# Token blocks of 512 columns in place of 464, and the two layers run one behind the other

## The chip, the cores and the metric

The kernel runs on one core of one Trainium2 chip. The metric is device time in microseconds (us), the median of 3 runs: 1123.47 us before the change (1122.75 to 1123.68). Where one execution was profiled, its own time is given beside it.

The engines in the text: PE is TensorE (matmuls; PEld is its weight load, which runs beside the matmuls), DVE is VectorE, ACT is ScalarE, POOL is GpSimd, SP is SyncE, whose queue issues every DMA of this kernel.

## The reference

Three stages over N = 6016 tokens with C = 256 channels and F = 2048 hidden columns:

```python
def _attn_ref(q, k, v, tau):                      # q, k, v: (1, 6016, 256)
    qn = q / (np.linalg.norm(q, axis=1, keepdims=True) + 1e-06)
    kn = k / (np.linalg.norm(k, axis=1, keepdims=True) + 1e-06)
    s = kn.transpose(0, 2, 1) @ qn / tau          # 256 x 256, sums over tokens
    a = softmax of s over its last axis
    return v @ a

def _moe_ref(x, w_in, w_out):                     # layer 0 of the kernel
    h = x @ w_in                                  # 6016 x 2048
    return (h - np.tanh(h)) @ w_out               # 6016 x 256

def _moe2_ref(x, w_in, w_out):                    # layer 1, with weights of its own
    h = x @ w_in
    g = np.where(h > 0.0, h, np.exp(np.minimum(h, 0.0)) - 1.0)
    return g @ w_out
```

The weights arrive as 8-byte floats. The kernel turns them into pairs of 4-byte numbers (a rounded high part and a rest), and does the same with every matmul operand, so that a product is three matmuls in the format fp32r: high by high, high by low, low by high.

## The kernel before

**Attention.** q and k are read once, their 256 x 256 product S is summed over tokens, and the softmax a is made from it. a is never applied to v: it is multiplied into layer 0's first weight matrix ("fold", the tiles `aw`), so layer 0 reads v directly.

**Blocks and units.** The tokens lie along the free dimension, in blocks of `width` = 464 columns: 12 of 464 and one of 448, 13 in all. For each layer and block there are NP = 8 units, p = 0 to 7, each for 256 of the 2048 hidden columns. A unit has 24 matmuls of one block's width: 12 that make h (`emit_h`, L404 by way of `product`) and 12 that add g @ w_out into the block's output o (`emit_out`, L572). Every matmul has a weight load of its own. Between them `emit_act` makes g on ACT and DVE: layer 0 with one tanh on ACT (L491) and a subtraction on DVE (L492), layer 1 with three ACT passes (L507 to L509) and two DVE passes (L511, L515). Both then take the high part (ACT L503, or DVE L501 and L519) and the rest (DVE L520).

**Order of the work.** The program is written out by hand in issue order; each engine runs its instructions in that order. The list `order` names the units. `LAG = 2`: on PE the out matmuls of a unit follow the h matmuls of the unit two later. h has two PSUM tiles in turn, so the h matmuls of a unit wait until DVE has read the h of two units before.

Before the change the first five p of blocks 0 and 1 alternate (`SIDE = NP - 3`), then come the rest of both, then block 2, and from there units of layer 1 for block b alternate with units of layer 0 for block b + 3 (`interleaved`). Three blocks of layer 1's input stay in SBUF as high and low parts (`xpool`, three buffers): `emit_evac` makes the high part on ACT (L588) and the rest on DVE (L589) from o in PSUM. Layer 0's own input comes by `load_v` from DRAM and is split by `split_v` (ACT L206, DVE L207).

**Conversions.** `Converter` runs beside the units, one weight piece per unit (two where `ticks` is 2): DMA, two ACT passes (L104, L105), four DVE passes (L121, L127, L133, L140), one ACT pass (L158) and one POOL pass (L165). The first converter ("early") has layer 0's weights and the first matrix of layer 1 in pieces of 512 columns, the second ("late") the last matrix of layer 1 in pieces of 256. Between them lies a switch: the SBUF room of the first is given to the second, so that the second's first DMA waits for the last POOL pass of the first, and an ACT pass on it stands in ACT's queue ahead of the unit's tanh.

**Fold.** From p = 1 on, the fold of a p (12 matmuls of 256 columns) stands in PE's queue shortly before the first unit that needs it.

Of the kernel before, what the change touches and what calls it, by code (L numbers as in the profile page):

```python
# [16 lines left out]
P = 128  # L17
# [5 lines left out]
def kernel(  # L23
# [25 lines left out]
    width = 464  # L49
# [17 lines left out]
    class Converter:  # L67
# [122 lines left out]

    v_of = {}

    def load_v(b):
        t0, n = blocks[b]
        raw = vpool.tile([P, KC, width], F32, tag="vraw", name=f"vraw{b}", bufs=1)
        nc.sync.dma_start(
            out=raw[:, :, :n], in_=vT[:, t0 : t0 + n].rearrange("(k p) t -> p k t", p=P)
        )
        v_of[b] = raw

    def split_v(b):
        _, n = blocks[b]
# [180 lines left out]
    with tc.manual_schedule():  # L383
# [5 lines left out]
        xpool = ctx.enter_context(tc.tile_pool(name="x", bufs=3, side="left"))  # L389
        gpool = ctx.enter_context(tc.tile_pool(name="g", bufs=2, side="left"))  # L390
        spool = ctx.enter_context(tc.tile_pool(name="s", bufs=2, side="left"))
        spool_e = ctx.enter_context(tc.tile_pool(name="e", bufs=1, side="left"))
# [46 lines left out]
        x_of = {}  # L439
# [20 lines left out]
        def emit_act(layer, b, p, h, ticks, fold):  # L460
# [43 lines left out]
            else:  # L504

                e = (late_pool[0] if late_pool else spool_e).tile([P, 2, width], F32, tag="e", name="e")[:, :, :n]
# [41 lines left out]
        def emit_last_evac(b):  # L548
            t0, n = blocks[b]
            o = o_of.pop((1, b))[:, :, :n]  # L550
            s = late_pool[0].tile([P, 2, width], F32, tag="osb", name="osb")[:, :, :n]
# [28 lines left out]
        def emit_evac(layer, b, p):  # L580
# [3 lines left out]
            o = o_of.pop((layer, b))[:, :, :n]  # L584
            if layer == 0:
# [3 lines left out]
                nc.vector.tensor_tensor(  # L589
                    out=x_lo[:, :, :n], in0=o, in1=x_hi[:, :, :n].bitcast(F32), op=ALU.subtract  # L590
                )
                x_of[b] = (x_hi, x_lo)
            else:
                s = late_pool[0].tile([P, 2, width], F32, tag="osb", name="osb")[:, :, :n]
                nc.scalar.activation(out=s, in_=o, func=AF.Copy)
# [4 lines left out]
        def interleaved(first, second, lead):  # L600

            first = [(*first, p) for p in range(NP)]
            second = [(*second, p) for p in range(NP)]
            units = []
            while first or second:
                if first:
                    units.append(first.pop(0))
                if second and (not first or len(first) <= NP - lead):
                    units.append(second.pop(0))
            return units  # L610


        order = [(0, b, p) for p in range(SIDE) for b in range(2)]
        order += [(0, b, p) for b in range(2) for p in range(SIDE, NP)]
        order += [(0, 2, p) for p in range(NP)]
        for b in range(NBLK - 3):
            order += interleaved((1, b), (0, b + 3), 1)
        order += interleaved((1, NBLK - 3), (1, NBLK - 2), 4)
        order += [(1, NBLK - 1, p) for p in range(NP)]

# [10 lines left out]
        for s, (layer, b, p) in enumerate(order):  # L631
            ticks = 1 + (s in (14, 18))
            if conv is not early and conv.done() and not late_pool:
                late_stack.close()
                pool = ctx.enter_context(tc.tile_pool(name="o", bufs=2, side="right"))
                late_pool.append(pool)
            if conv is early and early.done():
# [25 lines left out]
            if layer == 0 and b + 1 == nv and nv < NBLK:  # L663
                if p == 1:
                    load_v(nv)
                if p == (5 if b == 1 else 4):
                    split_v(nv)
                    nv += 1
# [38 lines left out]
```

## Time and profile before

| What | Before |
|---|---|
| device time, median of 3 runs | 1123.47 us |
| profiled execution, its own time | 1123.31 us |
| its span, first to last instruction | 1121.3 us |
| PE busy | 1109.8 us (99%), 5360 matmuls |
| DVE busy | 851.1 us (76%) |
| ACT busy | 554.9 us (49%) |
| mean granted TensorE clock | 0.998 of full speed |
| DMA | 42.30 MB, 38 GB/s on average |

How to read it: PE is the engine with almost no idle time, but its busy time counts matmuls with modelled ends that overlap, so it does not tell how fast the matmuls follow each other. That is read from their starts: the distance from one matmul's start to the next, called pace below. The other engines have idle time and matter only where PE waits for them. The profiled execution is 0.16 us under the median of the runs shown.

### The profile page before, as it was taken

The numbers are of one execution on the slowest core, as the hardware profiler recorded it, in microseconds if no ns is written. First come the engines' busy times: TensorE is split into PE (matmuls) and PEld (weight loads), VectorE is DVE, ScalarE is ACT, GpSimd is POOL, SyncE is SP. The second block draws the span as 40 slices with busy tenths as digits, with TensorE's granted clock in tenths as the row PEclk, the third lists the DMA queues.
The fourth block names the chain that finished last, engine by engine and source line by source line (L and its number), as shares of the span: only waits on it lengthen the run. The fifth ranks groups of instructions, "written<-read, shape, count | busy, mean of one in ns | idle before, by whom it ended". The sixth has DMA issues, their size and how long they took to land.

```text
span 1121.3 us, 13606 instructions
## 1 busy us (share of the span) xinstructions
PE 1109.8 (99%) x5360; PEld 992.0 (88%) x5360; DVE 851.1 (76%) x957; ACT 554.9 (49%) x662; POOL 75.0 (7%) x57
## 2 busy tenths in 40 slices
PE   9999999999999999999999999999999999999998
PEld 8789988888888888888888888888888889998897
DVE  6899997998666676667666776667766776678776
ACT  7776666664344334344444434443444443456564
POOL 6422212211000000000000000000000000000000
PEclk9999999999999999999999999999999999999999
DMA  9643221211001001001001001001000000000000
GB/s 350 238 130 92 78 73 57 69 43 34 1 1 35 1 1 35 1 1 34 1 1 34 1 1 34 1 1 35 1 23 12 1 18 1 1 18 1 7 28 17
DMA packets 23040, 42.30 MB, mean 38 GB/s; under 512 B 1984, under 2 KB 8896, under 8 KB 22976
## 3 DMA queue, kind: packets, MB, share of 16 engines
q1 hardware_dynamic: 22976, 41.43, 11.1%
q8 instruction: 42, 0.69, 0.3%
q14 instruction: 22, 0.18, 0.1%
HBM read 35.26 MB, written 6.16 MB: 37 GB/s over the span
## 4 chain that ended last, share of the span: by engine, by line
PE 89%; DVE 6%; issue 2%; ACT 2%; DMA 1%; SPq 0%; POOL 0%; ACTq 0%; DVEq 0%; POOLq 0%
PE h L404 42%; PE o L572 42%; PE S L247 3%; DVE glo L520 1%; PE aw L404 1%; DVE hz L121 1%; DVE cut L140 1%; DVE cut L127 1%; DMA qk<-in_k_dram 1%; DVE g L492 0%; ACT ghi L503 0%; DVE cut L133 0%; DVE g L515 0%; DVE xlo L589 0%; ACT g L491 0%
## 5 line engine op out<-in xcount | busy, mean ns | idle before, releaser
L511 DVE SCALAR_TENSOR_TENSOR g<-e,g 128x928 f32<-128x928 f32 (+1 forms) x103 | 116.8, 1134 | 197.2 <-ACT e L509 197.2
L507 ACT ACTIVATE e<-h 128x928 f32<-128x928 f32 (+1 forms) x103 | 97.3, 944 | 311.2 <-PE h L404 311.2
L520 DVE TENSOR_TENSOR glo<-g,ghi 128x928 fp32r<-128x928 f32 (+1 forms) x207 | 232.4, 1123 | 22.8 <-ACT ghi L503 3.1
L572 PE MATMUL o<-ghi,wout_hi 128*128 128x464 f32 (+1 forms) x832 | 208.8, 373 | 0.1
L572 PE MATMUL o<-glo,wout_hi 128*128 128x464 f32 (+1 forms) x832 | 208.7, 372 | 0.0
L572 PE MATMUL o<-ghi,wout_lo 128*128 128x464 f32 (+1 forms) x832 | 208.5, 372 | 0.0
L491 ACT ACTIVATE g<-h 128x928 f32<-128x928 f32 (+1 forms) x104 | 98.0, 943 | 162.9 <-PE h L404 162.8
L572 PEld LDWEIGHTS o<-glo,wout_hi 128*128 128x128 f32 x832 | 156.2, 188 | 18.9
L572 PEld LDWEIGHTS o<-ghi,wout_lo 128*128 128x128 f32 x832 | 156.3, 188 | 18.2
L572 PEld LDWEIGHTS o<-ghi,wout_hi 128*128 128x128 f32 x832 | 156.2, 188 | 17.7 <-ACT ghi L542 0.4
L404 PE MATMUL h<-vhi,win_hi 128*128 128x464 f32 (+1 forms) x416 | 154.6, 372 | 1.1 <-ACT win_hi L426 0.7
L404 PE MATMUL h<-vlo,win_hi 128*128 128x464 f32 (+1 forms) x416 | 155.1, 373 | 0.0
L404 PE MATMUL h<-xhi,win_hi 128*128 128x464 f32 (+1 forms) x414 | 153.9, 372 | 0.1
L404 PE MATMUL h<-xlo,win_hi 128*128 128x464 f32 (+1 forms) x414 | 153.6, 371 | 0.0
L515 DVE SCALAR_TENSOR_TENSOR g<-h,g 128x928 f32<-128x928 f32 (+1 forms) x103 | 115.5, 1122 | 10.0
L404 PE MATMUL h<-vhi,win_lo 128*128 128x464 f32 (+1 forms) x416 | 120.8, 371 | 0.0
L404 PE MATMUL h<-xhi,win_lo 128*128 128x464 f32 (+1 forms) x414 | 120.0, 370 | 0.0
L492 DVE TENSOR_TENSOR g<-h,g 128x928 f32<-128x928 f32 (+1 forms) x104 | 116.1, 1116 | 1.6 <-ACT g L491 1.4
L508 ACT ACTIVATE g<-e 128x928 f32<-128x928 f32 (+1 forms) x103 | 101.0, 981 | 3.3
L509 ACT ACTIVATE e<-e 128x928 f32<-128x928 f32 (+1 forms) x103 | 100.8, 978 | 3.3
L404 PEld LDWEIGHTS h<-vhi,win_hi 128*128 128x128 f32 x416 | 78.0, 188 | 11.2 <-ACT win_hi L426 0.9
L404 PEld LDWEIGHTS h<-vlo,win_hi 128*128 128x128 f32 x416 | 78.1, 188 | 9.6
(110 smaller groups left out, 1028.7 us busy)
## 6 DMA issues: line engine op xcount, KB each, us to landing
qk<-in_q_dram SPq DMA_DIRECT2D x23, 256.0 KB, 5.1
qk<-in_k_dram SPq DMA_DIRECT2D x23, 256.0 KB, 5.1
vraw<-in_vT_dram SPq DMA_DIRECT2D x12, 464.0 KB, 4.2
out_dram<-osb SPq DMA_DIRECT2D x12, 464.0 KB, 2.9
raw0in<-in_moe_w_in_dram SPq DMA_DIRECT2D x8, 512.0 KB, 3.8
raw0out<-in_moe_w_out_dram SPq DMA_DIRECT2D x8, 512.0 KB, 3.6
raw1in<-in_moe_w_in_dram SPq DMA_DIRECT2D x8, 512.0 KB, 3.7
raw1out<-in_moe_w_out_dram SPq DMA_DIRECT2D x16, 256.0 KB, 2.6
```

The source lines that it names most:

```text
L121: nc.vector.scalar_tensor_tensor(out=hz, in0=s["sq"], scalar=TINY_HIGH**2, in1=s["raw"][:, :, 1].bitcast(F32), op0=ALU.is_ge, op1=ALU.mult,)
L247: nc.tensor.matmul(out=S[m], lhsT=kk[:, 1, j, m * P : (m + 1) * P], rhs=qq[:, 0, j, :], start=(count[m] == 1), stop=(count[m] == total),)
L404: nc.tensor.matmul(out=out, lhsT=w, rhs=x, start=(i == 0), stop=(i == len(pairs) - 1))
L491: nc.scalar.activation(out=g, in_=h, func=AF.Tanh)
L492: nc.vector.tensor_tensor(out=g, in0=h, in1=g, op=ALU.subtract)
L507: nc.scalar.activation(out=e, in_=h, func=AF.Relu, scale=-1.0)
L508: nc.scalar.activation(out=g, in_=e, func=AF.Tanh, scale=-0.5)
L509: nc.scalar.activation(out=e, in_=e, func=AF.Exp, scale=-1.0)
L511: nc.vector.scalar_tensor_tensor(out=g, in0=e, scalar=1.0, in1=g, op0=ALU.add, op1=ALU.mult)
L515: nc.vector.scalar_tensor_tensor(out=g, in0=h, scalar=0.0, in1=g, op0=ALU.max, op1=ALU.add)
L520: nc.vector.tensor_tensor(out=lo, in0=g, in1=hi.bitcast(F32), op=ALU.subtract)
L572: nc.tensor.matmul(out=o[:, c, :n], lhsT=w[layer][:, f, c * P : (c + 1) * P], rhs=x[:, i], start=(f == 0 and w is wout_hi and x is hi), st ...
```

## The change

- `width` becomes 512, so there are 11 blocks of 512 columns and one of 384, 12 in all.
- The layers no longer alternate. `phases` lists all blocks of layer 0 and then all blocks of layer 1; `order` goes through them unit by unit, with blocks 0 and 1 still in pairs, now for all eight p.
- Layer 1's input isn't kept in SBUF. `emit_evac` copies o to an SBUF tile (ACT) and stores it to a DRAM tile `x_dram[b]`; `load_v` later reads it back in place of v, and `split_v` makes high and low part as for layer 0.
- The early converter has layer 0's weights alone, 16 pieces, one per unit; layer 1's 32 pieces of 256 columns all go through the late one, and the switch stands at unit 14. `ticks` is always 1.
- The pool `xpool` goes, the output tile gets a pool of its own with two buffers (`opool`), and the tile e of layer 1 takes two buffers in the room that the late converter leaves.

```diff
-    width = 464
+    width = 512
...
-    SIDE = NP - 3
-    starts = [2 * p if p < SIDE else p + SIDE for p in range(NP)]
+    starts = [2 * p for p in range(NP)]
...
-    NE = 8
-    early_units += [(1, "in", 2 * P * p, 2 * P) for p in range(NE)]
-    wanted = [(2 * p - 1, "in", p) for p in range(NE, NP)] + [(2 * p + 2, "out", p) for p in range(NP)]
     late_units = [
-        (1, which, 2 * P * p + P * i, P) for _, which, p in sorted(wanted) for i in range(2)
+        (1, which, 2 * P * p + P * i, P) for p in range(NP) for which in ("in", "out") for i in range(2)
     ]
...
+    phases = [(layer, b) for layer in range(2) for b in range(NBLK)]
+    dram = ctx.enter_context(tc.tile_pool(name="x", bufs=1, space=bass.MemoryType.DRAM))
+    x_dram = [dram.tile([P, KC, n], F32, name=f"x{b}") for b, (_, n) in enumerate(blocks)]
     v_of = {}
 
-    def load_v(b):
+    def load_v(i):
+        layer, b = phases[i]
         t0, n = blocks[b]
...
+        if layer == 0:
+            src = vT[:, t0 : t0 + n].rearrange("(k p) t -> p k t", p=P)
+        else:
+            src = x_dram[b]
+        nc.sync.dma_start(out=raw[:, :, :n], in_=src)
...
-            x_hi, x_lo = v_of[b] if layer == 0 else x_of[b]
+            x_hi, x_lo = v_of[layer * NBLK + b]
...
+            s = opool.tile([P, 2, width], F32, tag="osb", name="osb")[:, :, :n]
+            nc.scalar.activation(out=s, in_=o, func=AF.Copy)
             if layer == 0:
-                x_hi = xpool.tile([P, KC, width], F32R, tag="xhi", name=f"xhi{b}")
-                x_lo = xpool.tile([P, KC, width], F32R, tag="xlo", name=f"xlo{b}")
-                nc.scalar.activation(out=x_hi[:, :, :n], in_=o, func=AF.Copy)
-                nc.vector.tensor_tensor(
-                    out=x_lo[:, :, :n], in0=o, in1=x_hi[:, :, :n].bitcast(F32), op=ALU.subtract
-                )
-                x_of[b] = (x_hi, x_lo)
+                nc.sync.dma_start(out=x_dram[b], in_=s)
...
+        order = [(0, b, p) for p in range(NP) for b in range(2)]
+        order += [(layer, b, p) for layer, b in phases[2:] for p in range(NP)]
...
-            ticks = 1 + (s in (14, 18))
+            ticks = 1
...
+            if s == 3 or (s > 2 * NP and p == 1 and nv < len(phases)):
+                load_v(nv)
+            if s == 2 * NP - 2 or (s > 2 * NP and p == 4 and nv < len(phases)):
+                split_v(nv)
+                nv += 1
```

How the change moves instructions shows best at two places. The first is PE's queue in the middle of the program, around the first unit of block 5 in layer 0. In the names h0_5_0 is layer 0, block 5, p = 0, and o1_1 is the output of layer 1, block 1; the numbers behind the last underscore only count tiles. Before:

```order
L404 MATMUL h1_2_0_3174<-xhi2_1962,win_lo1_592 128x464 x2
L572 MATMUL o1_1_2703<-ghi_3132,wout_hi1_1758 128x464 x4
L572 MATMUL o1_1_2703<-ghi_3132,wout_lo1_1759 128x464 x4
L572 MATMUL o1_1_2703<-glo_3133,wout_hi1_1758 128x464 x4
L404 MATMUL h0_5_0_3213<-vhi5_2966,win_hi0_61 128x464
```

After (the same statements stand at L407 and L573):

```order
L407 MATMUL h0_4_7_2585<-vhi4_2111,win_lo0_62 128x512 x2
L573 MATMUL o0_4_2363<-ghi_2519,wout_hi0_63 128x512 x4
L573 MATMUL o0_4_2363<-ghi_2519,wout_lo0_64 128x512 x4
L573 MATMUL o0_4_2363<-glo_2520,wout_hi0_63 128x512 x4
L407 MATMUL h0_5_0_2631<-vhi5_2489,win_hi0_61 128x512
```

The neighbour of a layer 0 unit is now the layer 0 unit ahead of it, not one of layer 1, and every matmul has 512 columns; the pattern of 12 and 12 is the same. The second place is ACT's queue at the switch from the early to the late converter, with what each row waits for. Before, in block 2 of layer 0:

```order
L491 ACTIVATE g_1743<-h0_2_5_1718 128x928 [waits PE_49,Activation_49]
L158 ACTIVATE win_hi1_591<-cut_1669 128x2x256
L503 ACTIVATE ghi_1744<-g_1743 128x928 [waits DVE_49,PE_49]
L104 ACTIVATE sq_1772<-raw1out0_1766 128x256 [waits DMAHW5_49,Pool_49]
L105 ACTIVATE low_1773<-raw1out0_1766 128x256
L491 ACTIVATE g_1801<-h0_2_6_1776 128x928 [waits PE_49]
```

After, between the last units of blocks 0 and 1 (L429 is the fold's evacuation, L426 before; L492 the tanh; L504 the high part):

```order
L492 ACTIVATE g_1363<-h0_1_6_1325 128x1024 [waits PE_49]
L429 ACTIVATE win_hi0_61<-aw7_1338,rsum_78 128x256 [waits PE_49,Pool_49]
L429 ACTIVATE win_hi0_61<-aw7_1338,rsum_78 128x256
L158 ACTIVATE wout_hi0_63<-cut_1314 128x512 [waits DVE_49]
L504 ACTIVATE ghi_1364<-g_1363 128x1024 [waits DVE_49,PE_49]
L104 ACTIVATE sq_1396<-raw1in0_1390 128x256 [waits DMAHW4_49,DVE_49,Pool_49]
L105 ACTIVATE low_1397<-raw1in0_1390 128x256
L492 ACTIVATE g_1425<-h0_0_7_1400 128x1024 [waits PE_49]
```

In both the square pass of the late converter's first piece stands ahead of the next unit's tanh, one unit behind the last pass of the early converter; after the change two evacuations of the fold stand there too.

## Rows read from the trace of the kernel before

**Rows 1.** The page, part 1: busy time (share of the span) and instructions.

```profile
PE 1109.8 (99%) x5360; PEld 992.0 (88%) x5360; DVE 851.1 (76%) x957; ACT 554.9 (49%) x662; POOL 75.0 (7%) x57
```

**Rows 2.** The page, part 4: the chain that ended last, by engine.

```profile
PE 89%; DVE 6%; issue 2%; ACT 2%; DMA 1%; SPq 0%; POOL 0%; ACTq 0%; DVEq 0%; POOLq 0%
```

**Rows 3.** Waits of PE, whole span: total us, times, longest us.

```profile
PE aw L404 <- DVE g L492: 1.8, 1, 1.8
```

**Rows 4.** Waits of PE from 76 to 1110 us, all that there are.

```profile
PE h L404 <- DVE g L492: 0.4, 1, 0.4
```

**Rows 5.** The chain in order of time: start us, us, what.

```profile
213.97 2.53 PE o L572 x12
...
914.78 2.52 PE o L572 x12
```

**Rows 6.** Timeline of PE, the last block: start us, us, engine, line, instruction.

```profile
1087.27 0.37 PE L404 MATMUL h<-xhi,win_hi 128*128 128x448 f32 x1
...
1106.79 0.37 PE L404 MATMUL h<-xhi,win_hi 128*128 128x448 f32 x1
```

**Rows 7.** Timeline of PE around one fold.

```profile
84.80 0.28 PE L404 MATMUL aw<-win_hi,aT_hi 128*128 128x256 f32 x1
...
86.22 0.37 PE L572 MATMUL o<-ghi,wout_hi 128*128 128x464 f32 x1
```

**Rows 8.** Windows: length, busy of PE, PEld, DVE, ACT, POOL; PEclk, DMA, GB/s.

```profile
55.30:69.50 14.20, 14.18 (x72) 12.45 (x72) 13.64 (x21) 11.19 (x18) 3.91 (x3) 1.00 0.36 112
72.10:75.50 3.40, 3.40 (x15) 3.23 (x14) 3.37 (x6) 2.58 (x5) 0.00 (x0) 0.50 0.77 287
76.00:145.00 69.00, 69.00 (x357) 62.33 (x356) 66.74 (x85) 48.00 (x74) 15.47 (x12) 1.00 0.31 92
210.00:258.00 48.00, 48.00 (x230) 42.85 (x230) 46.79 (x74) 29.23 (x48) 9.60 (x9) 1.00 0.18 54
1020.00:1105.00 85.00, 85.00 (x410) 76.72 (x410) 67.75 (x69) 50.74 (x54) 0.00 (x0) 1.00 0.03 12
```

**Rows 9.** Timeline of PE behind its longest wait.

```profile
71.65 0.38 PE L404 MATMUL aw<-win_hi,aT_hi 128*128 128x256 f32 x1 [1.80 <-DVE g L492]
...
74.02 1.69 PE L572 MATMUL o<-ghi,wout_hi 128*128 128x464 f32 x4
75.55 0.80 PE L572 MATMUL o<-ghi,wout_lo 128*128 128x464 f32 x3
```

**Rows 10.** Groups by line and shape: busy us, mean ns of one, idle before.

```profile
L520 DVE TENSOR_TENSOR glo<-g,ghi 128x928 fp32r<-128x928 f32 x192 | 216.0, 1125 | 21.2 <-ACT ghi L503 3.1 <-DVE ghi L519 0.5
L511 DVE SCALAR_TENSOR_TENSOR g<-e,g 128x928 f32<-128x928 f32 x96 | 109.2, 1137 | 192.4 <-ACT e L509 192.4
L515 DVE SCALAR_TENSOR_TENSOR g<-h,g 128x928 f32<-128x928 f32 x96 | 107.9, 1124 | 9.3
L492 DVE TENSOR_TENSOR g<-h,g 128x928 f32<-128x928 f32 x96 | 107.4, 1119 | 1.6 <-ACT g L491 1.4
L519 DVE CAST ghi<-g 128x928 fp32r<-128x928 f32 x96 | 61.8, 644 | 9.2
L511 DVE SCALAR_TENSOR_TENSOR g<-e,g 128x896 f32<-128x896 f32 x7 | 7.7, 1093 | 4.7 <-ACT e L509 4.7
L127 DVE TENSOR_SCALAR cut<-hz 128x256 uint32<-128x256 uint32 x16 | 7.3, 456 | 0.0
```

**Rows 11.** Timelines of POOL and ACT at the switch.

```profile
177.83 1.30 POOL L165 TENSOR_TENSOR win_lo<-cut,win_hi 128x512 fp32r<-128x512 f32 x1 [3.25 <-ACT win_hi L158]
...
181.74 0.44 ACT L104 ACTIVATE sq<-raw1out 128x256 f32<-128x256 f32 x1 [1.90 <-DMA raw1out<-in_moe_w_out_dram]
```

**Rows 12.** The page, part 6: DMA, KB each, us from issue to landing.

```profile
vraw<-in_vT_dram SPq DMA_DIRECT2D x12, 464.0 KB, 4.2
out_dram<-osb SPq DMA_DIRECT2D x12, 464.0 KB, 2.9
```

More of the change, by code (lines that the diff above doesn't have):

```diff
@@ L188 @@
     rsum = aT_pool.tile([P, KC], F32, name="rsum")
+    phases = [(layer, b) for layer in range(2) for b in range(NBLK)]
+    dram = ctx.enter_context(tc.tile_pool(name="x", bufs=1, space=bass.MemoryType.DRAM))
+    x_dram = [dram.tile([P, KC, n], F32, name=f"x{b}") for b, (_, n) in enumerate(blocks)]
     v_of = {}
-    def load_v(b):
+    def load_v(i):
+        layer, b = phases[i]
         t0, n = blocks[b]
-        raw = vpool.tile([P, KC, width], F32, tag="vraw", name=f"vraw{b}", bufs=1)
-        nc.sync.dma_start(
-            out=raw[:, :, :n], in_=vT[:, t0 : t0 + n].rearrange("(k p) t -> p k t", p=P)
-        )
-        v_of[b] = raw
+        raw = vpool.tile([P, KC, width], F32, tag="vraw", name=f"vraw{i}", bufs=1)
+        if layer == 0:
[3 more added lines that the diff above has]
+        nc.sync.dma_start(out=raw[:, :, :n], in_=src)
+        v_of[i] = raw
     def split_v(b):
-        _, n = blocks[b]
+        _, n = blocks[phases[b][1]]
         raw = v_of[b]
@@ L388 @@
         win_lo[1] = wpool2.tile([P, KC, F], F32R, name="win_lo1")
-        xpool = ctx.enter_context(tc.tile_pool(name="x", bufs=3, side="left"))
         gpool = ctx.enter_context(tc.tile_pool(name="g", bufs=2, side="left"))
         spool = ctx.enter_context(tc.tile_pool(name="s", bufs=2, side="left"))
-        spool_e = ctx.enter_context(tc.tile_pool(name="e", bufs=1, side="left"))
+        opool = ctx.enter_context(tc.tile_pool(name="o", bufs=2, side="left"))
         ps_h = ctx.enter_context(tc.tile_pool(name="ps_h", bufs=2, space=PSUM))
@@ L504, in emit_act @@
             else:
-                e = (late_pool[0] if late_pool else spool_e).tile([P, 2, width], F32, tag="e", name="e")[:, :, :n]
+                e = late_pool[0].tile([P, 2, width], F32, tag="e", name="e")[:, :, :n]
                 nc.scalar.activation(out=e, in_=h, func=AF.Relu, scale=-1.0)
@@ L584, in emit_evac @@
             o = o_of.pop((layer, b))[:, :, :n]
+            s = opool.tile([P, 2, width], F32, tag="osb", name="osb")[:, :, :n]
+            nc.scalar.activation(out=s, in_=o, func=AF.Copy)
             if layer == 0:
-                x_hi = xpool.tile([P, KC, width], F32R, tag="xhi", name=f"xhi{b}")
-                x_lo = xpool.tile([P, KC, width], F32R, tag="xlo", name=f"xlo{b}")
-                nc.scalar.activation(out=x_hi[:, :, :n], in_=o, func=AF.Copy)
-                nc.vector.tensor_tensor(
-                    out=x_lo[:, :, :n], in0=o, in1=x_hi[:, :, :n].bitcast(F32), op=ALU.subtract
-                )
-                x_of[b] = (x_hi, x_lo)
-            else:
-                s = late_pool[0].tile([P, 2, width], F32, tag="osb", name="osb")[:, :, :n]
-                nc.scalar.activation(out=s, in_=o, func=AF.Copy)
+                nc.sync.dma_start(out=x_dram[b], in_=s)
+            else:
                 nc.sync.dma_start(
@@ L598, in emit_evac @@
                 )
[L600 to L619, printed above, removed]
+        order = [(0, b, p) for p in range(NP) for b in range(2)]
+        order += [(layer, b, p) for layer, b in phases[2:] for p in range(NP)]
         LAG = 2
@@ L631 @@
         for s, (layer, b, p) in enumerate(order):
-            ticks = 1 + (s in (14, 18))
+            ticks = 1
             if conv is not early and conv.done() and not late_pool:
                 late_stack.close()
-                pool = ctx.enter_context(tc.tile_pool(name="o", bufs=2, side="right"))
+                pool = ctx.enter_context(tc.tile_pool(name="e", bufs=2, side="right"))
                 late_pool.append(pool)
-            if conv is early and early.done():
+            if conv is early and early.done() and s >= starts[-1]:
                 right.close()
@@ L662 @@
                 emit_evac(*done[:3])
[L663 to L668, printed above, removed]
+            if s == 3 or (s > 2 * NP and p == 1 and nv < len(phases)):
[3 more added lines that the diff above has]
+                nv += 1
         for done in pend:
```

2 lines of the change are left out of this document (removed).

## The prediction

> **What bounds the kernel now.** I read the busy shares first: PE 99%, DVE 76%, ACT 49% [rows 1]. The chain that ended last agrees: 89% of the span runs over PE, 6% over DVE [rows 2]. Then the waits of PE, to see whether anyone else holds it up: in the layers it has one wait of 1.8 us near their start [rows 3], and from 76 to 1110 us one of 0.4 us in all [rows 4]. So the time is the number of matmuls times their pace, and what I need is the pace at each width, from starts.
>
> At 464 columns: two out groups start at 213.97 and 914.78 us [rows 5]; between them lie 139 units of 24 matmuls, so 700.81 / 3336 = 210.07 ns per matmul. At 448 columns: four units, 96 matmuls, from 1087.27 to 1106.79 us, 203.33 ns [rows 6]. At 256 columns: the 12 matmuls of one fold from 84.80 to 86.22 us, 118.3 ns [rows 7]. So the pace goes with the width; a weight load of fixed length does not set it, or the fold would be as slow as the rest. The granted clock is full in these stretches [rows 8], which at 2.4 GHz is one column per 0.4167 ns, and the rest is what a matmul costs beyond its columns: 210.07 - 193.33 = 16.7 ns at 464, 203.33 - 186.67 = 16.7 ns at 448, 118.3 - 106.7 = 11.6 ns at 256.
>
> **The pace, the main term.** The columns stay the same in sum (6016 tokens through the same weights). Before there are 12 x 2 x 192 = 4608 matmuls of 464 and 2 x 192 = 384 of 448 columns, together 4608 x 0.21007 + 384 x 0.20333 = 968.0 + 78.1 = 1046.1 us. After there are 11 x 2 x 192 = 4224 of 512 and 384 of 384: 384 fewer. No row has 512 columns. From below nothing can be faster than 512 x 0.4167 = 213.3 ns. From above: a straight line through the extras at 256 and 464 gives 17.9 ns, so 231.2 ns; the two nearest widths have the same extra, which gives 213.3 + 16.7 = 230.0 ns. I take 230.3, a quarter of the way up, since the flat stretch is much nearer than 256. For 384 columns the line gives 160 + 14.8 = 174.8 ns. After: 4224 x 0.2303 + 384 x 0.1748 = 972.8 + 67.1 = 1039.9 us, 6.2 us less. With 230.0 it is 7.5 us less, with 231.2 it is 2.4 us less.
>
> [...]
>
> **The start of the layers.** PE waits 1.8 us for DVE there [rows 3, 9]: the fold of p = 2 needs the h tile that the third unit's subtraction (L492) has still to read. Ahead of it PE runs 60 matmuls of block width from 55.3 us on, which become 60 x 0.0202 = 1.2 us longer. DVE is busy without a gap there (13.64 of 14.2 us, [rows 8]); six of its passes in that stretch are of block width (one split, three L492, two L520). A pass of 928 columns takes 1.137 us and one of 896 takes 1.093 (L511, [rows 10]), 1.4 ns per column, so at most 0.13 us more for 96 columns and by the other passes about 0.1: 0.6 us in sum. The wait goes from 1.8 to 1.2 us: -0.6. Right behind it the granted clock is 0.50 for 3.4 us [rows 8]: there the fold's 12 matmuls take 74.02 - 71.65 = 2.37 us against 1.42 at the full clock, and four out matmuls 75.55 - 74.02 = 1.53 against 0.84 [rows 9], a loss of 1.6 us. I leave it in the sum; should the shorter wait leave the clock alone, it goes.
>
> **The switch of the converters.** The 0.4 us wait [rows 4] falls into the stage where two conversions stand in one unit; with `ticks` at 1 it goes, -0.4. What comes is the order at the switch: the square pass waits for a DMA that waits for POOL, and the tanh of the unit stands behind it on ACT. Before, POOL ended at 179.13 and the square began at 181.74, 2.6 us later, ACT having waited 1.9 us [rows 11], and PE did not wait [rows 4]. After, count from the end of the h matmuls of unit 13: the fold ends at 1.4, its two evacuations and L158 at about 3.1, POOL at 4.5, the square begins at 7.1, the tanh about 0.9 later, at 8.0, against 1.4 + 2 x 2.76 + 0.2 = 7.1 without it. Behind it DVE has L492, the rest of the conversion, L520 and the split of block 2's low part, which ends near 14.4; PE asks for that at 15.4. So it costs nothing, with 1.0 us to spare; at worst, with the DMA 2 us late, 1 us. I take 0.
>
> **Layer 1 on its own.** Now a layer 1 unit no longer has a lighter layer 0 unit beside it. Per unit DVE has three passes of at most 1.137 + 0.132 = 1.27 us and a cast of about 0.71 [rows 10], 4.5 us, and an eighth of a split, 0.16: 4.7 us of the unit's 24 x 0.2303 = 5.53. That is 85%; the last block before, layer 1 alone as well, had DVE at 67.75 of 85 us, 80%, without PE waiting [rows 4, 8]. The chain must fit too: h ends, three ACT passes to about 3.3 us, L511 and L515 to 5.8; PE wants that h tile 3 groups of 12 later, at 8.3. Hidden.
>
> **The late conversions in layer 0.** They now run for 32 units. DVE has two passes of 1.25, a cast of 0.7, four conversion passes of about 0.45 [rows 10] and the split: about 5.2 of 5.53 us, 93%. Before, from 210 to 258 us, it was 46.79 of 48 us, 97%, and PE did not wait [rows 4, 8]. In the paired stage before it DVE was at 66.74 of 69 us [rows 8]; after, the block-wide passes add 0.5 us and PE 1.0 us for each pair. Lighter in both: nothing lost.
>
> **The way through DRAM.** It adds 12 stores and 12 loads, and 12 ACT copies of about 1.0 us. A store lands in some 2.9 us and a load in some 4.2 [rows 12]. A block's load is issued at p = 1 of the block ahead of it and split at p = 4, three units or 16.6 us later; the store it reads is eleven blocks old. ACT stands in that wait ahead of the next unit's first pass, so a load late by over 12 us would hold PE; what else is on the queue then is one store and, up to block 6, the pieces of the conversion. Hidden, 0. The splits of blocks 0 and 1 ahead of the layers become longer by 0.1 us each: +0.2, at worst.
>
> **Sum.** 1123.31 - 6.2 - 0.6 - 0.4 + 0.2 = 1116.3 us for an execution like the profiled one; the median of the runs shown is 0.16 us above that one, which I leave out. The tail (last h, two output groups, copies, store) is left as it is.
>
> **Rivals.**
> The extra grows along the line: 231.2 ns at 512, so 3.8 us more than the forecast, 1120.1 us. For it: the extra did grow from 256 to 448. Against: not from 448 to 464.
>
> Slower: a full stream of 512 columns costs another step. The extra went up by 5.1 ns somewhere between 256 and 448 columns, no row shows one above 464, and the 512 columns fill a half of the h tile to its end, which no matmul did before. Another such step gives 21.8 ns, 235.1 ns, 4224 x 0.0048 = 20.3 us over the forecast: 1136.6 us. The point from which it decides is a pace of 231.9 ns, where the gain is gone. Against it stands the flat stretch.
>
> DVE becomes the bound in layer 1: from 5.53 us of passes per unit on, each 0.1 us more costs 96 x 0.1 = 9.6 us. At 5.6 us that is 1123.0 us. Against it: 85%.
>
> [...]
>
> **How the numbers follow.** Forecast 1116.3 us, 64%; its own range is 1113.5 (230.0 ns and no stretch at half clock) to 1119 (the switch costs 1 us, another 1.6 us of half clock). The line, 18%. The step, 9%. DVE, 5%. The page's pace, 4%. A difference under 0.2%, 2.2 us, can't be told from no change: 1121.2 to 1125.7 us. Faster: 64 + about 12 of the line's 18 + 4 = 80%. Same: the rest of the line's, most of DVE's: 10%. Slower: the step and the rest of DVE's, 10%. The range 1112.5 to 1122.5 leaves out the page's pace, the step and half of DVE's.
>
> **What would show it.** Starts of 512-column matmuls 230 to 231 ns apart, 12 of them in 2.76 us, in both layers alike; 384-column ones 175 ns apart. A wait of PE of about 1.2 us at the first fold with p = 2, a short stretch at half clock behind it, and none over 1 us at unit 16. DVE at about 85% in layer 1, with PE not waiting. The forecast is wrong if the pace is off by 1 ns (4.2 us), or if PE waits for DVE, ACT or a load in every unit or block.

## The result, and the profile after the change

| What | Before | After |
|---|---|---|
| device time, median of 4 runs each, taken in turns | 1123.2 us (1122.75 to 1123.68) | 1107.99 us (1107.85 to 1108.23) |
| profiled execution, its own time | 1123.31 us | 1107.92 us |
| its span | 1121.3 us | 1106.1 us |
| mean granted TensorE clock | 0.998 | 0.999 |

The ratio is 0.9865, with a 95% interval of 0.9853 to 0.9877. The change is faster, by 15.2 us (1.35%). The forecast was 1116.3 us with a range down to 1112.5: the sign was right, and the gain more than twice the 7.0 us forecast.

The page of the kernel after the change, part 1 (to be read against [rows 1]) and the chain that ended last by engine (against [rows 2]):

```profile
PE 1094.0 (99%) x4976; PEld 913.2 (83%) x4976; DVE 843.2 (76%) x931; ACT 564.2 (51%) x663; POOL 72.0 (7%) x65
PE 95%; DVE 2%; ACT 1%; DMA 1%; SPq 0%; issue 0%; DVEq 0%; ACTq 0%
```

There are the 384 matmuls fewer that the change leaves out. The chain now runs over PE for 95% of the span where it was 89%: no other engine has come to hold PE up for long.

All waits of PE from 60 us on, except one of 0.4 us in the last unit (total us, times, longest us); they answer to [rows 3, 4]:

```profile
PE aw L407 <- DVE g L493: 1.3, 1, 1.3
PE h L407 <- ACT low L105: 0.5, 1, 0.5
```

The first is the start wait, which the prediction had at 1.2 us. The second comes 5 us behind it, in the paired stage, and is new; from 85 us to the last unit there is none. At the switch of the converters ACT does wait for the late converter's first DMA, for 2.7 us (the waits of ACT from 60 to 145 us), and PE does not notice:

```profile
ACT sq L104 <- DMA raw1in<-in_moe_w_in_dram: 2.7, 1, 2.7
```

Next come windows of the kernel after (length, busy of PE, PEld, DVE, ACT, POOL; PEclk, DMA share, GB/s): the place where PE had run at half clock, the late conversions in layer 0, and layer 1. They answer to [rows 8]:

```profile
72.10:75.50 3.40, 3.35 (x21) 3.02 (x22) 3.37 (x5) 3.09 (x6) 0.28 (x1) 1.00 0.86 305
210.00:258.00 48.00, 48.00 (x214) 39.75 (x213) 39.27 (x62) 19.96 (x38) 6.67 (x9) 1.00 0.23 72
600.00:1050.00 450.00, 450.00 (x1951) 366.30 (x1950) 365.48 (x337) 275.95 (x266) 0.00 (x0) 1.00 0.07 24
```

PE is busy without a gap in the last two. DVE is at 39.27 of 48 us (82%) beside the late conversions and at 365.48 of 450 (81%) in layer 1, and nobody waits for it. The granted clock in the first window is 1.00; before it was 0.50.

A DVE pass of 1024 columns in layer 1 (a group by line and shape, against [rows 10]), and the DMAs of the new way through DRAM (KB each, us from issue to landing, against [rows 12]):

```profile
L512 DVE SCALAR_TENSOR_TENSOR g<-e,g 128x1024 f32<-128x1024 f32 x81 | 99.2, 1225 | 58.4 <-ACT e L510 58.4
```

```profile
x<-osb SPq DMA_DIRECT2D x11, 512.0 KB, 2.9
vraw<-x SPq DMA_DIRECT2D x11, 512.0 KB, 3.9
```

A DVE pass became 0.09 us longer (1137 to 1225 ns), not 0.13. The way through DRAM takes 2.9 us out and 3.9 us back and is hidden.

So the time is matmuls times pace, as before. This is the chain in order of time (start us, us, what), whose pieces here are groups of 12 matmuls: two rows of layer 0, four of layer 1, and two of the 384-column block (against [rows 5]):

```profile
198.70 2.72 PE h L407 x12
...
535.98 2.72 PE h L407 x12
...
565.74 2.08 PE o L573 x12
567.82 2.08 PE h L407 x12
...
588.63 2.81 PE o L573 x12
591.44 2.73 PE h L407 x12
...
1051.26 2.73 PE h L407 x12
1053.99 2.81 PE o L573 x12
```

From 198.70 to 535.98 us lie 62 units of 24 matmuls: 337.28 / 1488 = 226.67 ns a matmul. The 384-column block goes at 2.08 / 12 = 173.33 ns: 128 columns fewer take 53.3 ns less, 0.4167 ns a column, the figure that the prediction used. 512 columns at that rate are 213.3 ns, and 13.3 ns of the 226.67 lie beyond them, as at 384 columns by the same reckoning. I call that the extra. From 588.63 to 1053.99 lie 84 units: 465.36 / 2016 = 230.83 ns. There the two kinds differ: the h matmuls take 2.73 / 12 = 227.5 ns, the out matmuls 2.81 / 12 = 234.2 ns, an extra of about 21. The prediction had 230.3 ns in both layers alike.

So the forecast's largest term had the wrong size, and there was a riddle: why is 512 columns cheaper by 3.4 ns per matmul than 464 and 448 had led one to expect, why only in one layer, and only for one kind of matmul in the other?

### The profile page after: what moved, and what is told of

It is laid out like the page before. It is cut to its first block, busy times and chain, and to the rows that moved or that the text cites. A ratio compares the mean times of both kernels' runs of the same rounds, so it can differ in the third digit from the quotient of the medians.

```text
span 1106.1 us, 12902 instructions
## 1 busy us (share of the span) xinstructions
PE 1094.0 (99%) x4976; PEld 913.2 (83%) x4976; DVE 843.2 (76%) x931; ACT 564.2 (51%) x663; POOL 72.0 (7%) x65
## 4 chain that ended last, share of the span: by engine, by line
PE 95%; DVE 2%; ACT 1%; DMA 1%; SPq 0%; issue 0%; DVEq 0%; ACTq 0%
PE o L573 46%; PE h L407 46%; PE S L251 3%; PE aw L407 1%; DMA qk<-in_k_dram 1%; DVE glo L521 0%; DVE cut L140 0%; SPq L270 0%; DVE cut L133 0%; DVE cut L127 0%; SPq L271 0%; DVE root L334 0%; ACT low L105 0%; DVE g L539 0%; ACT sq L104 0%
## 5 line engine op out<-in xcount | busy, mean ns | idle before, releaser
L407 PE MATMUL h<-vhi,win_hi 128*128 128x512 f32 (+1 forms) x766 | 295.4, 386 | 1.2 <-ACT win_hi L429 0.7
L407 PE MATMUL h<-vlo,win_hi 128*128 128x512 f32 (+1 forms) x766 | 295.0, 385 | 0.0
L521 DVE TENSOR_TENSOR glo<-g,ghi 128x1024 fp32r<-128x1024 f32 (+1 forms) x191 | 229.9, 1204 | 25.2 <-ACT ghi L504 6.4
L492 ACT ACTIVATE g<-h 128x1024 f32<-128x1024 f32 (+1 forms) x96 | 97.0, 1010 | 290.3 <-PE h L407 290.3
L407 PE MATMUL h<-vhi,win_lo 128*128 128x512 f32 (+1 forms) x766 | 232.9, 385 | 0.0
L493 DVE TENSOR_TENSOR g<-h,g 128x1024 f32<-128x1024 f32 (+1 forms) x96 | 115.4, 1202 | 121.8 <-ACT g L492 121.7
L573 PE MATMUL o<-ghi,wout_hi 128*128 128x512 f32 (+1 forms) x768 | 205.1, 388 | 0.4 <-ACT ghi L543 0.4
L573 PE MATMUL o<-glo,wout_hi 128*128 128x512 f32 (+1 forms) x768 | 204.5, 388 | 0.0
L573 PE MATMUL o<-ghi,wout_lo 128*128 128x512 f32 (+1 forms) x768 | 204.1, 387 | 0.0
L407 PEld LDWEIGHTS h<-vhi,win_hi 128*128 128x128 f32 x766 | 143.9, 188 | 30.7 <-ACT win_hi L429 0.9
L573 PEld LDWEIGHTS o<-ghi,wout_lo 128*128 128x128 f32 x768 | 143.7, 188 | 30.3
L573 PEld LDWEIGHTS o<-glo,wout_hi 128*128 128x128 f32 x768 | 143.8, 188 | 29.8
L512 DVE SCALAR_TENSOR_TENSOR g<-e,g 128x1024 f32<-128x1024 f32 (+1 forms) x95 | 114.5, 1205 | 69.6 <-ACT e L510 69.6
L407 PEld LDWEIGHTS h<-vlo,win_hi 128*128 128x128 f32 x766 | 143.8, 188 | 28.2
L573 PEld LDWEIGHTS o<-ghi,wout_hi 128*128 128x128 f32 x768 | 142.9, 188 | 28.7 <-ACT ghi L543 0.7
L407 PEld LDWEIGHTS h<-vhi,win_lo 128*128 128x128 f32 x766 | 143.4, 188 | 27.8 <-DVE win_lo L435 0.4
```

Source lines behind the costliest of these rows:

```text
L407: nc.tensor.matmul(out=out, lhsT=w, rhs=x, start=(i == 0), stop=(i == len(pairs) - 1))
L492: nc.scalar.activation(out=g, in_=h, func=AF.Tanh)
L493: nc.vector.tensor_tensor(out=g, in0=h, in1=g, op=ALU.subtract)
L512: nc.vector.scalar_tensor_tensor(out=g, in0=e, scalar=1.0, in1=g, op0=ALU.add, op1=ALU.mult)
L521: nc.vector.tensor_tensor(out=lo, in0=g, in1=hi.bitcast(F32), op=ALU.subtract)
L573: nc.tensor.matmul(out=o[:, c, :n], lhsT=w[layer][:, f, c * P : (c + 1) * P], rhs=x[:, i], start=(f == 0 and w is wout_hi and x is hi), st ...
```

## Experiments

In all of them the extra of a matmul is its start-to-start time less its columns at 0.4167 ns each, the cost of a column between 384 and 512 in the changed kernel. Bytes of a place are those of the compiled program, within a partition.

### Which part of the change it is: width, rows or order

**Width alone undone.** `width = 512` becomes `width = 464`; all the rest of the change stays.

```diff
-    width = 512
+    width = 464
```

Expected: 

> The changed kernel with blocks of 464 columns again, all else as changed (layers one behind the other, DRAM tile, one conversion per unit). It asks whether the low extra per matmul (13.3 ns over the columns in layer 0 at 512, against 16.7 at 464 before) belongs to the width or to the new order. Theory width (or the row distance that goes with it): extra in layer 0 about 16.5 ns, pace about 210 ns, time 1120 to 1123 us. Rival order (a layer on its own disturbs PE less than two that alternate): extra 13.3 ns, pace 206.7 ns, time 1104 to 1112 us.

Measured: 1123.03 us (ratio to before 0.9996, 0.9986 to 1.0005). The order of the layers, the way through DRAM and the other edits are worth nothing in sum; a cost of one that another's gain makes up for is not excluded. The gain comes only with `width = 512`.

**Blocks of 464 in tiles made for 512.** With 512 columns the rows of a tile also move apart, from 1856 to 2048 bytes. Here the blocks have 464 columns and the rows stay 2048 bytes apart.

```diff
-    width = 512
-    blocks = [(t, min(width, N - t)) for t in range(0, N, width)]
+    block, width = 464, 512
+    blocks = [(t, min(block, N - t)) for t in range(0, N, block)]
```

Expected: 

> Blocks of 464 columns in tiles whose rows stay 512 columns (2048 bytes) apart, in the changed order. Theory rows: the extra comes from rows that begin 1856 bytes apart, so with 2048 it is 13.3 ns, pace 206.7 ns, time about 1105 us. Rival width: the number of columns of the matmul itself sets it, extra 16.5 ns, pace 210 ns, time 1120 to 1123 us, as with rows of 464.

Measured: 1120.58 us (1119.82 to 1121.2; ratio 0.9971, 0.996 to 0.9982). The rows bring 2.5 us. The chain shows where, with a group of each kind in layer 0 and in layer 1:

```profile
302.76 2.51 PE o L573 x12
305.27 2.51 PE h L407 x12
...
804.58 2.55 PE o L573 x12
807.12 2.51 PE h L407 x12
```

Between distant starts layer 0 goes at 208.9 ns in place of 210.07, and layer 1's out matmuls are again slower than its h matmuls. So that difference does not need 512 columns.

### What slows the out matmuls of layer 1: where their weights lie

In the changed kernel every operand of PE on the left side of SBUF begins at a multiple of 128 bytes. The second layer's output weights and the ACT tile e are on the right side, which is filled downward from the top, and begin 96 bytes past one. (The weights are at byte 196576, which is 96 past a multiple of 128, before the change as well.)

**The right side moved by 96 bytes.** An unused tile is put at its top:

```diff
+    pad = ctx.enter_context(tc.tile_pool(name="pad", bufs=1, side="right"))
+    pad.tile([P, 24], F32, name="pad")
     early = Converter(
```

Expected: 

> The changed kernel with an unused tile of 96 bytes at the right end of SBUF, so that the second out matrix of layer 1 and the tile e, which begin 32 bytes past a multiple of 64, begin at a multiple of 128; nothing else moves. In the changed kernel out matmuls of 512 columns have an extra of 20.7 ns in layer 1 and 13.3 in layer 0. Theory place: the 32 bytes cause it; the extra in layer 1 falls to 13.3 ns (h from 14.3 to 13.3), 1056 x (7.4 + 1.0) ns = 8.9 us less, time about 1099 us. Rival load: three ACT passes per unit beside the out matmuls cause it, whatever their place; extra stays 20.7 ns, time 1108 us.

Measured: **1099.19 us** (1099.07 to 1100.0; ratio 0.9784, 0.9769 to 0.9799). An unused tile of 96 bytes is worth 8.8 us. Layer 1 now has layer 0's pace, for both kinds:

```profile
588.57 2.72 PE o L575 x12
591.29 2.72 PE h L409 x12
```

**The left side moved by 32 bytes instead**, away from the multiples of 128:

```diff
+    pad = ctx.enter_context(tc.tile_pool(name="pad", bufs=1, side="left"))
+    pad.tile([P, 8], F32, name="pad")
```

Expected: 

> The counterpart: an unused tile of 32 bytes at the left end, so that all tiles of layer 0 and the shared ones (weights, v, ghi, glo, g) begin 32 bytes past a multiple of 64. Theory place: the extra in layer 0 rises from 13.3 ns towards 20 ns, 2112 matmuls x up to 7 ns = up to 15 us more, time 1113 to 1123 us. Rival load: nothing changes, 1108 us.

Measured: 1108.77 us (1108.63 to 1108.9). Layer 0, with all its operands 32 bytes past a multiple of 128, keeps its pace; layer 1 (second pair of rows), whose output weights now lie 64 bytes off the other operands, is about as slow as in the changed kernel:

```profile
305.17 2.72 PE o L575 x12
307.89 2.72 PE h L409 x12
...
805.34 2.80 PE o L575 x12
808.14 2.75 PE h L409 x12
```

So a multiple of 128 is nothing in itself. Two tiles had moved at once on the right side; the next two runs part them.

**Only e moved to a multiple of 128.** The unused tile is put between the weights and e.

```diff
+                pad2 = ctx.enter_context(tc.tile_pool(name="pad2", bufs=1, side="right"))
+                pad2.tile([P, 24], F32, name="pad2")
                 pool = ctx.enter_context(tc.tile_pool(name="e", bufs=2, side="right"))
```

Expected: 

> Layer 1's tile e of the three ACT passes is moved to a multiple of 128 bytes (96 unused bytes ahead of it), the second layer's output weights stay 32 bytes past a multiple of 64. Theory A (the place of the weights that PE loads costs the 7.4 ns more of the out matmuls of layer 1, the place of e the 1.0 ns more of its h matmuls): the h matmuls of layer 1 go to 226.7 ns, the out matmuls stay at 234, 1108.0 - 1056 x 1.0 ns = 1106.9 us. Theory B (what costs is ACT's passes through e beside the matmuls): both go to 226.7 ns, 1099.2 us.

Measured: 1107.76 us (2 runs, 1107.54 and 1107.99), as in the changed kernel: theory B falls.

**Only the output weights moved.** The 96 bytes at the top stay in, and 32 more ahead of e (`pad2` with 8 columns) put it back to 96 past a multiple.

Expected: 

> The second layer's output weights are moved to a multiple of 128 bytes, e stays 32 bytes past a multiple of 64 (as in the changed kernel). Theory A (weights cost the out matmuls): out matmuls of layer 1 at 226.7 ns, h matmuls at 227.7, 1108.0 - 1056 x 7.4 ns = 1100.2 us. Theory B (ACT's passes through e cost): no change, 1108.0 us.

Measured: 1099.35 us (2 runs, 1099.19 and 1099.5). The weights account for all of it, and e for nothing. Theory A had given the 1.0 ns on layer 1's h matmuls to e; that part is wrong, since it goes and comes with the output weights too: where the out groups are slower, the h groups between them are slower as well. A group of each kind in layer 1, first with e moved, then with the weights moved:

```profile
804.36 2.81 PE o L573 x12
807.17 2.73 PE h L407 x12
```

```profile
803.57 2.72 PE h L409 x12
806.29 2.72 PE o L575 x12
```

**The right side moved by 64 bytes**: the weights lie 32 past a multiple of 128, the left side at the multiples. The tile at the top has 16 columns in place of 24.

Expected: 

> 64 unused bytes ahead of all tiles on the right side: e and the second layer's output weights lie 32 bytes past a multiple of 128, where the run with the left tiles shifted had its layer 0 weights at no loss; in the changed kernel they lie 96 past it. Theory C (any place off the grid of the other operands costs): out matmuls of layer 1 stay above 230 ns, 1106 to 1108 us. Theory D (32 bytes past a multiple of 128 is as good as the multiple, 96 is not): all matmuls of 512 columns at 226.7 ns, 1099.2 us.

Measured: 1107.18 us (1107.06 and 1107.31). Theory D falls: out groups of layer 1 take 2.79 us, 232.5 ns.

```profile
804.75 2.79 PE o L575 x12
```

The weights of layer 0 lay at this same place, 32 past, without loss when the left side was moved as a whole.

**Both sides moved, to 32 past a multiple of 128.** 8 columns on the left and 16 on the right.

Expected: 

> 32 unused bytes ahead of the left side and 64 ahead of the right one: every operand of every matmul of both layers lies 32 bytes past a multiple of 128, the second layer's output weights too, at the place where they cost 19.5 ns in the run with the right side alone moved. Theory G (what counts is where the second layer's output weights lie against the other operands): all matmuls of 512 columns at 226.7 ns, 1099.2 us, with 0.5 us more for the rest as in the run with the left side moved. Theory H (these weights must lie at a multiple of 128 in themselves): out matmuls of layer 1 above 230 ns, 1107 us.

Measured: 1099.3 us (1099.2 and 1099.4). In layer 1:

```profile
803.58 2.72 PE h L411 x12
806.30 2.72 PE o L577 x12
```

The same weights at the same bytes cost 19 ns extra when the left side is at the multiple and 13.3 when it is 32 past it. What counts is where the operands of PE lie **relative to each other**, modulo 128 bytes; theory H falls.

**The moving operand of the out matmuls moved to its weights' place.** ghi and glo (with g and osb behind them) go 96 past a multiple, where layer 1's output weights are.

```diff
+        padg = ctx.enter_context(tc.tile_pool(name="padg", bufs=1, side="left"))
+        padg.tile([P, 24], F32, name="padg")
         gpool = ctx.enter_context(tc.tile_pool(name="g", bufs=2, side="left"))
```

Expected: 

> 96 unused bytes ahead of the moving operands of the out matmuls (ghi, glo) alone: in layer 1 they lie with the output weights, 96 bytes past a multiple of 128; in layer 0 the output weights are at a multiple of 128 and ghi, glo 96 past it. Theory G1 (weights against the moving operand of the same matmul): out matmuls of layer 1 fall from 234 to 226.7 ns, those of layer 0 rise to about 234, and the time stays at 1108. Theory G2 (output weights against input weights, or weights at all): no change in either layer, 1108. Theory H (each weight tile by itself): no change either.

Measured: 1119.06 us (ratio 0.9963, 0.9948 to 0.9978), 11 us slower than the changed kernel, which none of the theories had; its four runs lie within 0.3 us. Two groups of layer 0 and two of layer 1:

```profile
301.83 2.76 PE h L409 x12
304.59 2.81 PE o L575 x12
...
805.21 2.77 PE o L575 x12
807.98 2.77 PE h L409 x12
```

Layer 0's out matmuls rise to 234.2 ns, as G1 said, with their weights untouched. But layer 1's fall only to 230.8 although their two operands now agree, and the h matmuls, whose operands agreed all along, rise to 230 in both layers. So one matmul's own pair is not the whole of it: one kind of matmul whose operands lie elsewhere slows its neighbours too.

The single starts say how far. An h group of layer 0 in this run, from its first matmul to its tenth to the out group behind it (start us, us, engine, line, instruction):

```profile
301.67 0.40 PE L409 MATMUL h<-vhi,win_hi 128*128 128x512 f32 x1
...
303.75 0.39 PE L409 MATMUL h<-vlo,win_hi 128*128 128x512 f32 x1
...
304.43 1.10 PE L575 MATMUL o<-ghi,wout_hi 128*128 128x512 f32 x4
```

The first nine take 2.08 / 9 = 231 ns, the last three 0.68 / 3 = 226.7. Averaged over the groups between 620 and 1040 us, layer 1's out matmuls do the same: 231.9 ns over the first nine, 226.7 at the tenth and eleventh. In the changed kernel only the first two h matmuls of a group in layer 1 (232.7 and 230.8 ns) and the last (228.2) leave the full pace. But the out matmuls of layer 0 here, whose own two operands disagree, stay at 230.9 ns or more at all twelve places. That fits theory G1 with something it did not have: after each change of place between two kinds, matmuls whose own operands agree need some time to come back to the full pace.

A whole layer went at the full pace only where all operands of PE in it shared one place modulo 128 bytes. g and osb, which DVE and ACT use, moved along with ghi and glo here, and no run parts them. Rows 1856 bytes apart put every second row of a moving operand 64 bytes past a multiple of 128, so the 2.5 us of the rows may be a cost of the same kind; that is not shown. What brings this about, no run shows: in the changed kernel the pace of the out matmuls moves by 7.5 ns, from 226.7 in layer 0 to 234.2 in layer 1, while the profile's weight loads last 188 ns on average in layer 0 (198.7 to 536 us) and 188 to 189 ns in layer 1 (600 to 1050 us).

### What a matmul costs beyond its columns, by width

**Many widths in one kernel**, with the right side in place:

```diff
-    blocks = [(t, min(width, N - t)) for t in range(0, N, width)]
+    sizes = [512, 512, 496, 480, 480, 464, 464, 448, 448, 416, 384, 384, 320, 208]
+    blocks = [(sum(sizes[:i]), n) for i, n in enumerate(sizes)]
```

Expected: 

> Tiles placed as in the run with the right side at multiples of 128 bytes, but blocks of 512, 512, 496, 480, 480, 464, 464, 448, 448, 416, 384, 384, 320 and 208 columns in place of eleven of 512 and one of 384: what a matmul costs beyond its columns, read at each width from the starts in layer 0 and layer 1. Theory E (one fixed extra at every width once all tiles lie well): 13.3 ns at each of them. Theory F (13.3 ns only where the width is a multiple of 128): 13.3 at 512 and 384, 15 to 18 at the others, 15.6 at 464. The line of my prediction would be 17.9 at 464 and falling to about 14 at 320, which the runs at 384 (13.3) speak against.

Measured (one run): 1122.02 us. The chain, one group each of 496, 480, 464, 448, 416, 384, 512, 320 and 208 columns:

```profile
174.47 2.64 PE o L576 x12
...
221.62 2.60 PE o L576 x12
...
304.11 2.52 PE o L576 x12
...
391.22 2.43 PE h L410 x12
...
453.33 2.24 PE h L410 x12
...
523.64 2.08 PE o L576 x12
...
633.75 2.72 PE o L576 x12
...
1083.99 1.76 PE h L410 x12
...
1097.22 1.33 PE h L410 x12
```

A hundredth of a us is 0.8 ns here.

| columns | 512 | 496 | 480 | 464 | 448 | 416 | 384 | 320 | 208 |
|---|---|---|---|---|---|---|---|---|---|
| ns from start to start (us / 12) | 226.7 | 220.0 | 216.7 | 210.0 | 202.5 | 186.7 | 173.3 | 146.7 | 110.8 |
| extra, ns | 13.3 | 13.3 | 16.7 | 16.7 | 15.8 | 13.3 | 13.3 | 13.3 | 24.2 |

Neither theory E nor F: 496 is no multiple of 128 and has 13.3. 512 and 320 columns are 80.0 ns apart, 0.4167 ns a column in this kernel too, and 496, 416 and 384 lie on the line between them. At the widths tried from 320 to 512 columns the extra is flat at 13.3, with a **hump** from 448 to 480. Single starts are evenly apart at 512 and 496; at 464 they alternate between 205 and 215 ns in this run. Both block widths of the kernel before lie on the hump.

**Two splits of the same tokens.** Both have 4608 matmuls, as many as the kernel of 11 x 512 and 384, and the right side in place; only the widths differ. First `sizes = [512] * 4 + [496] * 8`:

Expected: 

> Right side at multiples of 128, blocks of 4 x 512 and 8 x 496 columns: 4608 matmuls, as many as with 11 x 512 and 384. By the paces of the run with mixed widths (13.3 ns beyond the columns at 512, 496 and 384 alike) 1099.2 us, with the tail's last block longer by 0.3 us: 1099.5. By theory F (13.3 only at multiples of 128, 16.7 elsewhere) 3072 x 3.3 ns more: 1109.5.

Measured: 1098.66 us (1098.38 to 1098.91; ratio 0.9781, 0.9767 to 0.9796). Then `sizes = [512] * 8 + [480] * 4`:

Expected: 

> The same with 8 x 512 and 4 x 480 columns: again 4608 matmuls and the same columns in sum. By the paces of the run with mixed widths (16.7 ns at 480) 1536 x 3.3 ns = 5.1 us over the run with 496, 1104.5 us. If one extra per matmul held at all widths, no difference to the run with 496, 1099.5. By the line of the prediction (extra growing with the width) less than that run.

Measured: 1103.79 us (1103.57 to 1104.59; ratio 0.9828, 0.9812 to 0.9845). The 5.1 us between the two are the 1536 x 3.3 ns of the table: the hump is real in the time too.

**464 columns with everything in place**: the second kernel above (blocks of 464, rows of 2048 bytes) with the 96 bytes at the top of the right side.

Expected: 

> Blocks of 464 columns in tiles whose rows are 2048 bytes apart, and the right side at multiples of 128 bytes. If the place of the output weights costs layer 1 what it costs at 512: out matmuls of layer 1 from 18.6 to 15.6 ns beyond their columns, as in layer 0, h matmuls from 15.9 to 15.6, so 1120.6 - 1152 x 3.3 ns = 1116.8 us, and the width alone then is worth 1116.8 - 1099.2 = 17.6 us. If 464 goes at 16.6 ns as in the run with mixed widths, where its tiles lay as well, layer 0 becomes slower and layer 1's out matmuls go to 16.6: about 1120.6 us, no change.

Measured: 1116.28 us (median of 8 runs; seven of them 1115.96 to 1117.12, one 1122.38, which nothing on record explains). Layer 1's two kinds go alike, and at layer 0's pace:

```profile
802.29 2.51 PE o L575 x12
804.80 2.51 PE h L409 x12
```

That is 208.9 ns, an extra of 15.6; in the kernel with mixed widths, with the same places and the same rows of 2048 bytes, 464 columns had 16.7, so the rhythm on the hump is not always the same, and what sets it is open. Against the kernel with 512 columns in place, 1099.19 us, the width alone is worth 17.1 us.

### The stretch at half clock

The clock stayed full behind the start wait in the changed kernel. The wait had become shorter, 1.3 us in place of 1.8, but the columns ahead of it had become more as well.

**The wait lengthened alone.** In the kernel with the right side in place, the third unit gets one more DVE pass ahead of the subtraction that PE waits for:

```diff
+                if b == 0 and p == 1:
+                    nc.vector.tensor_copy(out=spare, in_=h[:, 0, :448])
                 nc.vector.tensor_tensor(out=g, in0=h, in1=g, op=ALU.subtract)
```

Expected: 

> Right side at multiples of 128 bytes, blocks of 512, and one more DVE pass ahead of the subtraction of the third unit: a copy of 448 columns of its h tile to a tile that nothing reads, about 0.65 us by DVE's passes of 512 columns there (0.65 to 0.69 us). PE's wait at the first fold with p = 2 grows from 1.2 to about 1.9 us. If the length of that wait decides on the clock: a stretch of 3.4 us at a granted clock of 0.50 behind it, as in the kernel before (wait 1.8), and 1099.2 + 0.65 + 1.6 = 1101.4 us. If the width decides (more columns ahead of the wait): the clock stays full, 1099.9 us.

Measured: 1100.0 us (1099.65 to 1100.65). The wait of PE, and the window behind it:

```profile
PE aw L410 <- DVE g L498: 1.9, 1, 1.9
```

```profile
73.80:77.20 3.40, 3.39 (x21) 3.08 (x22) 3.24 (x6) 3.14 (x5) 0.00 (x0) 1.00 0.76 287
```

The clock is full in this execution, the one that was profiled. It is full too with 464 columns in place, behind a wait of 1.8 us (first fence), and 0.50 with 464 columns and the right side not in place, behind the same wait (second fence):

```profile
PE aw L409 <- DVE g L495: 1.8, 1, 1.8
72.00:75.40 3.40, 3.39 (x21) 3.21 (x22) 3.37 (x5) 3.00 (x6) 0.34 (x1) 1.00 0.86 292
```

```profile
PE aw L407 <- DVE g L493: 1.8, 1, 1.8
73.20:76.60 3.40, 3.40 (x12) 2.95 (x11) 3.40 (x5) 3.09 (x6) 1.04 (x1) 0.50 0.65 212
```

But single executions do not settle this, for the stretch comes and goes with one and the same kernel. In the three profiles that have it (the kernel before, the width undone, blocks of 464 in tiles made for 512) the mean granted clock of the execution is 0.998; in the other thirteen it is 0.999 or 1.000. This mean is on record for the runs without a profile too:

| kernels | wait of PE in the profile, us | runs with a mean clock of 0.998 |
|---|---|---|
| before (beside the experiments) | 1.8 | 24 of 39 |
| width undone | 1.8 | 5 of 10 |
| 464 columns in tiles made for 512 | 1.8 | 4 of 8 |
| the same, right side in place | 1.8 | 3 of 8 |
| 512 columns, the wait lengthened alone | 1.9 | 1 of 4 |
| the changed kernel and the ten others | 1.1 to 1.3 | none of 31 |

So the shorter wait does go with a full clock, as my prediction had thought it might, while the longer one does not bring the stretch each time. Not shown are that the wait does it by itself (the one kernel that parts it from the width has a single run of four) and what decides from run to run.

In the kernel before, the 24 runs have a median of 1123.84 us and the other 15 one of 1122.86: the stretch costs 1.0 us net. The 1.6 us that the prediction read from the rows are not all lost, since with the clock full PE comes early to its next wait: the thirteen profiles without the stretch have a wait of 0.4 to 0.6 us for ACT behind it (`PE h <- ACT low`), the three with it have none.

## Why the prediction was wrong

**What held.** PE is the bound and its pace times the number of matmuls is the time. The start wait was forecast at 1.2 us and is 1.3. The switch costs PE nothing, and the 0.4 us wait of before has gone, though another of 0.5 us has come behind the start wait, which the account did not have. The prediction said that the stretch at half clock would go if the shorter wait left the clock alone; it has gone. DVE hides in layer 1 (81%, forecast 85%) and beside the late conversions (82%, forecast 93%). The way through DRAM is hidden. With the width undone the time was that of before to 0.1%, so these edits come to nothing in sum. Apart from the stretch, none of this moves the sum by over 0.5 us.

**The step that failed** is the pace: "the two nearest widths have the same extra, which gives 213.3 + 16.7 = 230.0 ns", raised to 230.3 towards the line. It is 226.67 ns in layer 0 and 230.83 in layer 1, 228.75 on average: 4224 x 1.55 ns = 6.5 us less than forecast. At 384 columns 173.3 in place of 174.8 is another 0.6 us. The stretch at half clock, which the sum kept, has gone: 1.6 us. Together that is 8.7 us; the new wait of 0.5 us, which goes with the full clock, leaves 8.2, and the miss was 8.3.

**Why that step failed.** I read two neighbouring widths with the same extra as a flat stretch that goes on. Both stand on one hump, and 512 lies beyond it; the fold's 11.6 ns at 256 columns [rows 7] was the sign that lower extras exist, and I used it only to draw a line that rises. That the two agreed so well was in part chance: the 448 was read in the last block, layer 1 alone, whose output weights lie off, and in place 448 columns take 202.5 ns in place of 203.33. Nor need all of the 16.7 ns at 464 belong to the width: with the rows 2048 bytes apart and the weights in place, 464 columns take 208.9 ns in one kernel, 1.2 ns less than [rows 5] show, though 210.0 in another. The forecast's demand, "in both layers alike", also failed: layer 1's mean of 230.83 happens to be near the forecast, but it is made of 227.5 and 234.2, and it is what misplaced weights cost, not what 512 columns cost.

**The rivals.** The line (231.2 ns) is refuted by 496 and 512 columns in place. The step was looked for above 464 columns; there is one, but it lies below, between 416 and 448, and leads down again at 496. DVE did not become the bound. No run shows the term behind the last 4% of the chances: at 512 columns the lowest pace is 226.67 ns, and the lowest median of a kernel here is 1098.66 us. The 213.3 ns from below, the columns alone at 0.4167 ns, was my estimate; no run came nearer to it than those 226.67. My range left out everything below 1112.5 because I held the extra at 464 as a floor for the extra at 512, with no row that said so.

## What to carry to other kernels

Where PE is the bound, read the pace per kind of matmul and per stage, not one mean: a difference between two kinds with the same columns is a cost with a cause, and here a 96-byte unused tile took 8.8 us away (1107.99 to 1099.19). Look at where PE's operands begin, weights and moving ones, and give them one place modulo 128 bytes within a stage. Do not carry an extra per matmul from two widths to a third: try the width, since 16 columns more or less (480 or 496) were worth 5 us of 1100 at the same number of matmuls.

## What had not been expected of the hardware

- The place of PE's operands relative to each other changes the pace, with no wait in the profile: 226.7 ns with all of them at one place modulo 128 bytes, 234.2 for out matmuls whose weights lie 96 bytes off, 232.5 at 32 bytes off, and up to 230.8 on average for neighbours whose own operands agree, which come back to the full pace within their group.
- What a matmul costs beyond its columns is not monotone in the width: 13.3 ns at 320 to 416, 15.8 to 16.7 at 448 to 480, 13.3 at 496 and 512, and 24.2 at 208.
- Behind a wait of PE of 1.8 us, 3.4 us at a granted clock of 0.50 came in some runs of a kernel and not in others: by the mean clock, in 24 of 39 runs of the kernel before, and in none of 31 runs of kernels whose wait was 1.1 to 1.3 us.
